# Result in four parts on two quadrants of two banks, V63 ending in parts of 8 keys, two pieces of K per VectorE instruction: a decode attention kernel on Trainium2

## The chip, the cores and the metric

One core of one Trainium2 chip. The metric is the device time of one execution in microseconds (us). The kernel before takes 1288.92 us (median of 3 runs, 1288.82 to 1288.93). Each kernel was also taken once with the hardware profiler; a profile's span is about 1.8 us shorter than the device time of the same execution.

## The reference, cut to what matters

```python
xn = layernorm(x)                                    # x: 4 x 512, one token for each of 4 batches
q  = (xn @ wq)                                       # 32 heads of 128
s  = einsum("bhqd,bhkd->bhqk", q, k_cache) * 128**-0.5   # 8192 keys a head
o  = einsum("bhqk,bhkd->bhqd", softmax(s), v_cache)
out = x + o.reshape(4, 1, 4096) @ wo + (silu(xn @ w_gate) * (xn @ w_up)) @ w_down
```

k_cache and v_cache are 4 x 32 x 8192 x 128 in bfloat16, 268 MB each. Everything is read once: 551 MB.

## The kernel before

The K and V caches go through five SBUF slots of 4 MB, one tile for two heads of one batch: 64 tiles K0 to K63 and 64 tiles V0 to V63. A stage i transposes K tile i on VectorE, multiplies it with q on TensorE (scores), takes the softmax of two tiles at a time, and multiplies V tile i - 2 with the probabilities (PV). wo takes one slot from stage 57 on. The parts that matter, with cuts marked:

```python
def t_piece(n, g):                       # one of 8 pieces of a K tile
    kt = kt_pool.tile([P, w], ...)       # 5 buffers
    nc.vector.transpose(out=kt..., in_=k_tiles[n][:, g * w:(g + 1) * w]...)
def s_piece(n, g):                       # 4 matmuls of 512 columns on that piece
    ...
# stage i, i < 64
for g in range(NTG):
    t_piece(i, g); s_piece(i, g)
...
# the parts in which V tiles are loaded
load_v(nv, (32, 32, 32, 16, 16) if nv == NT - 1 else (32,) * 4 if nv == NT - 2 else (T,))
...
# the last stage: V63, 128 keys, one matmul a key for batch 3, summed in xps
pv_last(xps, range(T // 2))
fin_2(H // HT - 1, xps, nb=B - 1, start=False)   # adds batches 0 to 2, from o_acc by ScalarE and VectorE
pv_last(xps, range(T // 2, T))
fin_3(H // HT - 1, xps)                          # otn, VectorE
...
def wo_mm(i):                                    # head i: 2 matmuls of 256 columns
    for half in range(2):
        mm(yo_ps[half][0:B, :], otn[:, i, :], wo_t[0][...half...], start=False)
...
nc.vector.tensor_copy(out=res[0][:], in_=yo_ps[0][0:B, :])
nc.sync.dma_start(out=out_flat[:, 0:DH], in_=res[0][:])
nc.scalar.copy(out=res[1][:], in_=yo_ps[1][0:B, :])
nc.scalar.dma_start(out=out_flat[:, DH:D], in_=res[1][:])
```

## Time and profile before

| | before |
|---|---|
| device time, median | 1288.92 us |
| span of the profile | 1287.1 us |
| TensorE / VectorE busy | 84% / 57% |
| DMA share, 100 to 1200 us | 1.00, 432 GB/s |
| last V part lands (chain of waits) | 1282.67 us |
| from there to the end of the span | 4.4 us |

The prediction below shows the page, the stretches and the timeline of the end, and says how to read each.

### The profile page before, as it was taken

How to read it: one execution, taken by the hardware profiler on the slowest of the kernel's cores; microseconds unless marked ns; L12 is line 12 of the kernel's file. 1: busy time of each engine (PE TensorE's matmuls, PEld its weight loads, DVE VectorE, ACT ScalarE, POOL GpSimd, SP SyncE). 2: the span in 40 equal slices, each digit the busy share in tenths (PEclk: the TensorE clock that was granted, in tenths of full speed). 3: DMA queues.
4: the chain of work that ended last, by engine and by line, in shares of the span. 5: the costliest groups of instructions: out<-in, count | busy, mean ns of one | idle time of the engine just before them, and what ended most of it. 6: DMA issues, size and time to landing. Idle time of an engine off the chain costs nothing.

```text
span 1287.1 us, 11189 instructions
## 1 busy us (share of the span) xinstructions
PE 1083.1 (84%) x4778; PEld 430.3 (33%) x4778; DVE 738.1 (57%) x951; ACT 39.7 (3%) x87; POOL 5.3 (0%) x13
## 2 busy tenths in 40 slices
PE   4888888888888798897997888888887988978788
PEld 1334333333333333332333333333333333333334
DVE  6663556546556556466556566465465465573544
ACT  1000000000000000000000000000000000000000
POOL 1000000000000000000000000000000000000000
PEclk9898898998989999898998989989899898989899
DMA  9999999999999999999999999999999999999997
GB/s 407 427 430 435 437 425 437 429 436 431 432 435 428 436 432 433 431 432 435 431 435 428 434 432 431 436 431 433 430 434 431 437 430 432 433 431 427 433 434 304
DMA packets 21529, 551.49 MB, mean 428 GB/s; under 512 B 2268, under 2 KB 2792, under 8 KB 3944
## 3 DMA queue, kind: packets, MB, share of 16 engines
q1 hardware_dynamic: 21464, 550.78, 99.4%
q8 instruction: 37, 0.61, 0.2%
q14 instruction: 12, 0.10, 0.0%
q10 hardware_dynamic: 16, 0.01, 0.0%
HBM read 550.77 MB, written 0.00 MB: 428 GB/s over the span
## 4 chain that ended last, share of the span: by engine, by line
DMA 50%; PE 31%; DVE 14%; issue 5%; ACT 1%; SPq 0%; DVEq 0%
DMA slot<-in_A_k_cache_dram 44%; PE oacc L76 17%; PE sps L76 12%; DVE kt L277 11%; DMA slot<-in_A_v_cache_dram 6%; PE mps L76 1%; DVE ptz L318 1%; DVE o L356 1%; PE xps L76 1%; DVE o_sb L354 1%; ACT o_sb L353 0%; PE mps L299 0%; DVE otn L377 0%; PE yo_ps L76 0%; DVE rcp L328 0%
## 5 line engine op out<-in xcount | busy, mean ns | idle before, releaser
L76 PE MATMUL sps<-kt,zq 128*128 128x512 bf16 x2048 | 578.3, 421 | 145.2 <-DVE kt L277 128.7
L277 DVE STREAM_TRANSPOSE kt<-slot 128x1024 uint32<-128x1024 uint32 x512 | 587.6, 1210 | 90.4 <-DMA slot<-in_A_k_cache_dram 89.5
L76 PE MATMUL oacc<-slot,ptz 128*8 128x512 bf16 x2016 | 450.4, 379 | 0.4 <-DMA slot<-in_A_v_cache_dram 0.4
L76 PEld LDWEIGHTS <-zq 128*128 128x128 bf16 x2048 | 212.0, 104 | 496.1 <-issue 317.0
L76 PEld LDWEIGHTS <-ptz 128*8 128x8 bf16 x2016 | 177.5, 92 | 258.1 <-issue 27.8
L328 DVE RECIPROCAL rcp<-mps 128x4 f32<-128x4 f32 x32 | 5.9, 183 | 281.9 <-PE mps L76 281.9
L354 DVE TENSOR_TENSOR o_sb<-o_sb,rowu 128x512 f32<-128x512 f32 x16 | 11.1, 693 | 89.2 <-ACT o_sb L353 89.0
L76 PE MATMUL xps<-rowy,o 128*32 128x4 f32 (+1 forms) x228 | 13.5, 205 | 37.3 <-DVE o L356 37.3
L293 DVE TENSOR_REDUCE mx<-sps 128x1 f32<-128x512 f32 x32 | 22.1, 692 | 18.5 <-PE sps L76 18.5
L76 PEld LDWEIGHTS xps<-rowy,o 128*32 128x32 f32 (+1 forms) x228 | 12.1, 154 | 44.9 <-DVE o L356 44.9
L268 DVE COPY zq<-qt 32x8 bf16<-32x8 bf16 x128 | 21.3, 166 | 1.3
L302 DVE TENSOR_REDUCE nm<-mps 128x4 f32<-128x64 f32 x32 | 7.2, 225 | 24.0 <-PE mps L299 24.0
L356 DVE TENSOR_REDUCE o<-o_sb 128x128 f32<-128x512 f32 x16 | 16.3, 1020 | 0.5
L76 PEld LDWEIGHTS mps<-rowb,rs 128*128 128x128 f32 x64 | 9.5, 186 | 13.8 <-issue 13.8
L76 PEld LDWEIGHTS <-slot 128*128 128x128 bf16 x272 | 11.7, 126 | 3.5 <-DVE slot L188 2.6
L76 PE MATMUL mps<-rowb,rs 128*128 128x4 f32 x64 | 12.3, 263 | 0.0
L353 ACT COPY o_sb<-oacc 128x512 f32<-128x512 f32 x16 | 9.4, 586 | 76.8 <-PE oacc L76 76.8
L377 DVE TENSOR_TENSOR otn<-xps,rcp 32x16 bf16<-32x16 f32 x28 | 4.8, 170 | 11.7 <-PE xps L76 10.3
L299 PE MATMUL mps<-ident_f,mx 128*128 128x128 f32 x32 | 10.3, 323 | 0.8 <-DVE mx L293 0.8
L299 PEld LDWEIGHTS mps<-ident_f,mx 128*128 128x128 f32 x32 | 4.3, 133 | 14.7 <-DVE mx L293 14.2
L170 PE MATMUL xps<-ident,kt 4*128 4x4 bf16 x4 | 0.3, 173 | 10.1 <-DVE kt L165 10.1
L76 PE MATMUL yo_ps<-slot,otn 128*4 128x256 bf16 x64 | 8.2, 281 | 0.3 <-DVE otn L366 0.3
(150 smaller groups left out, 148.5 us busy)
## 6 DMA issues: line engine op xcount, KB each, us to landing
slot<-in_A_k_cache_dram SPq DMA_DIRECT2D x64, 4096.0 KB, 39.2
slot<-in_A_v_cache_dram SPq DMA_DIRECT2D x62, 4096.0 KB, 36.8
slot<-in_A_v_cache_dram SPq DMA_DIRECT2D x7, 1024.0 KB, 22.3
slot<-in_A_wq_dram SPq DMA_DIRECT2D x1, 4096.0 KB, 12.3
slot<-in_A_wo_dram SPq DMA_DIRECT2D x1, 3584.0 KB, 40.2
slot<-in_B_w_gate_dram SPq DMA_DIRECT2D x1, 1792.0 KB, 31.9
slot<-in_B_w_up_dram SPq DMA_DIRECT2D x1, 1792.0 KB, 35.8
slot<-in_B_w_down_dram SPq DMA_DIRECT2D x1, 1792.0 KB, 30.9
```

The costliest lines, as they stand in the source:

```text
L76: nc.tensor.matmul(out_ap, lhsT=lhsT, rhs=rhs, start=start, stop=True, skip_group_check=True, **kw)
L268: nc.vector.tensor_copy(out=zq[gr % 2][a * QB:(a + 1) * QB, :, :, XO + a * QB].rearrange("p b (j r) -> p r j b", r=2), in_=qt[a * QB:(a + ...
L277: nc.vector.transpose(out=kt[:].bitcast(dt.uint32).rearrange("p (j t r) -> p t j r", j=2, r=QB), in_=src.rearrange("p (t j r) -> p t j r", ...
L293: nc.vector.reduce_max(out=mx[:], in_=s_ps[gr][:], axis=AX.X)
L299: nc.tensor.matmul(mps[:, 0:P], lhsT=nmx.pop(gr)[:, 0:1].to_broadcast([P, P]), rhs=ident_f[:, :], is_transpose=True, start=True, stop=True ...
L302: nc.vector.tensor_reduce(out=nm[:], in_=by_row(mps[:, 0:P]), axis=AX.XY, op=ALU.max, negate=True)
L318: nc.vector.transpose(out=t_[y * HP:(y + 1) * HP, :, y, :, :].rearrange("p s u x -> p s (u x)"), in_=p_[y * HP:(y + 1) * HP, :].rearrange( ...
L328: nc.vector.reciprocal(out=rcp[j][:, :, 2 * bp:2 * bp + 2], in_=mps[:, P:P + B].rearrange("p (y b) -> p y b", y=HT))
L353: nc.scalar.copy(out=o_sb[:].rearrange("p u d -> p (u d)"), in_=o_acc[j % 2][:])
L354: nc.vector.tensor_tensor(out=o_sb[:], in0=o_sb[:], in1=rowu[:].unsqueeze(2).to_broadcast([P, NV, Dh]), op=ALU.mult)
L356: nc.vector.reduce_sum(out=o1[:], in_=o_sb[:].rearrange("p u d -> p d u"), axis=AX.X)
L377: nc.vector.tensor_tensor(out=otn[q0:q1, blk * 4:blk * 4 + 4, :], in0=xps[q0:q1], in1=r_[q0:q1, y, :].unsqueeze(1).to_broadcast([QB, 4, B] ...
```

## The change

Its intent: shorten the serial end (fewer keys behind the last landing, two overlapping quadrants for the result product, narrower rounding copies on two engines) and save VectorE the fixed cost of half of its transposes (0.15 us each by the prediction's estimate). Buffers are cut to make room. The diff, cut to its core:

```diff
+    ND = 2
-    kt_pool = ctx.enter_context(tc.tile_pool(name="ktp", bufs=5))
+    kt_pool = ctx.enter_context(tc.tile_pool(name="ktp", bufs=3))
 ...
-    yo_ps = [psY.tile([B, DH], dt.float32, name="yo_ps") for _ in range(2)]
+    DH, DQ = D // 2, D // 4
+    yo_ps = [psY.tile([2 * QB, DQ], dt.float32, name="yo_ps") for _ in range(2)]   # and zeroed
+    def yo_mm(lhsT, rhs, start):
+        for i in range(2):
+            for a in range(2):
+                c0 = a * DH + i * DQ
+                mm(yo_ps[i][a * QB:a * QB + B, :], lhsT, rhs[:, c0:c0 + DQ], start=start)
 ...
-    def t_piece(n, g):
+    def t_piece(n, g, nd):          # nd pieces in one transpose
 ...
-        p_ = pp.tile([P, 512], dt.bfloat16, name="p_")
+        p_ = pp.tile([P, 512], dt.bfloat16, name="p_", bufs=1)      # o_sb likewise
 ...
-            load_v(nv, (32, 32, 32, 16, 16) if nv == NT - 1 ...
+            load_v(nv, (32, 32, 32, 16, 8, 8) if nv == NT - 1 ...
 ...
-            for g in range(NTG):
-                t_piece(i, g)
-                s_piece(i, g)
+            nd = 1 if i >= NT - 2 else ND
+            for k in range(0, NTG, nd):
+                t_piece(i, k, nd)
+                for g in range(k, k + nd):
+                    s_piece(i, g)
 ...
-    (the two copies and two stores shown above)
+    res = persist.tile([2 * QB, DH], dt.bfloat16, name="res")
+    nc.vector.tensor_copy(out=res[:, 0:DQ], in_=yo_ps[0][:])
+    nc.scalar.copy(out=res[:, DQ:DH], in_=yo_ps[1][:])
+    nc.sync.dma_start(out=out_flat[:, 0:DH], in_=res[0:B, :])
+    nc.scalar.dma_start(out=out_flat[:, DH:D], in_=res[QB:QB + B, :])
```

More of the change, by code (lines that the diff above doesn't have):

```diff
@@ L203 @@
     otn = persist.tile([P, H, B], dt.bfloat16, name="otn")
-    DH = D // 2
-    yo_ps = [psY.tile([B, DH], dt.float32, name="yo_ps") for _ in range(2)]
+    DH, DQ = D // 2, D // 4
+    yo_ps = [psY.tile([2 * QB, DQ], dt.float32, name="yo_ps") for _ in range(2)]
+    for y_ in yo_ps:
+        nc.vector.memset(y_[:], 0.0)
+    def yo_mm(lhsT, rhs, start):
[3 more added lines that the diff above has]
+                mm(yo_ps[i][a * QB:a * QB + B, :], lhsT, rhs[:, c0:c0 + DQ], start=start)
     ffn = {}
@@ L240, in do_ffn @@
         nc.vector.tensor_tensor(out=yfx[:], in0=yf_ps[0:B, :], in1=xf[:], op=ALU.add)
-        for j in range(2):
-            mm(yo_ps[j][0:B, :], ident_f[0:B, 0:B], yfx[:, j * DH:(j + 1) * DH], start=True)
+        yo_mm(ident_f[0:B, 0:B], yfx[:], True)
     NB4 = H // 4
@@ L270, in build_q @@
                 in_=qt[a * QB:(a + 1) * QB, half, :, hh * 2:hh * 2 + 2, cg * B + bp * 2:cg * B + bp * 2 + 2])
-    def t_piece(n, g):
+    def t_piece(n, g, nd):
         w = TG * Dh
-        kt = kt_pool.tile([P, w], dt.bfloat16, name="kt")
-        src = k_tiles[n][:, g * w:(g + 1) * w].bitcast(dt.uint32)
-        nc.vector.transpose(out=kt[:].bitcast(dt.uint32).rearrange("p (j t r) -> p t j r", j=2, r=QB),
+        kt = kt_pool.tile([P, ND * w], dt.bfloat16, name="kt")
+        src = k_tiles[n][:, g * w:(g + nd) * w].bitcast(dt.uint32)
+        nc.vector.transpose(out=kt[:, 0:nd * w].bitcast(dt.uint32).rearrange("p (j t r) -> p t j r", j=2, r=QB),
                             in_=src.rearrange("p (t j r) -> p t j r", j=2, r=QB))
-        kts[n, g] = kt
+        for i in range(nd):
+            kts[n, g + i] = kt[:, 0:nd * w].rearrange("p (j n r) -> p j n r", j=2, r=2)[:, :, i * 512:(i + 1) * 512, :]
     def s_piece(n, g):
@@ L284, in s_piece @@
             s_ps[gr] = psS.tile([P, 512], dt.float32, name="sps")
-        kt = kts.pop((n, g))[:].rearrange("p (j n r) -> p j n r", j=2, r=2)
+        kt = kts.pop((n, g))
         off = XO - 2 * (bb * NTG + g)
@@ L351, in fin_1 @@
     def fin_1(j):
-        o_sb = pp.tile([P, NV, Dh], dt.float32, name="o_sb")
+        o_sb = pp.tile([P, NV, Dh], dt.float32, name="o_sb", bufs=1)
         nc.scalar.copy(out=o_sb[:].rearrange("p u d -> p (u d)"), in_=o_acc[j % 2][:])
@@ L380, in wo_mm @@
     def wo_mm(i):
-        for half in range(2):
-            mm(yo_ps[half][0:B, :], otn[:, i, :], wo_t[0][:, i * D + half * DH:i * D + (half + 1) * DH], start=False)
+        yo_mm(otn[:, i, :], wo_t[0][:, i * D:(i + 1) * D], False)
     NK = T // NV
@@ L394 @@
         if 0 <= nv < NT:
-            load_v(nv, (32, 32, 32, 16, 16) if nv == NT - 1 else (32,) * 4 if nv == NT - 2 else (T,))
+            load_v(nv, (32, 32, 32, 16, 8, 8) if nv == NT - 1 else (32,) * 4 if nv == NT - 2 else (T,))
         if i == R_FFN - 3:
@@ L403 @@
         if i < NT:
-            for g in range(NTG):
-                t_piece(i, g)
-                s_piece(i, g)
-                if g == 0 and bb == 0 and gr > 0:
+            nd = 1 if i >= NT - 2 else ND
[3 more added lines that the diff above has]
+                    s_piece(i, g)
+                if k == 0 and bb == 0 and gr > 0:
                     pt_turn(gr - 1)
@@ L453 @@
     assert wo_next == H
-    res = [persist.tile([B, DH], dt.bfloat16, name=f"res{j}") for j in range(2)]
-    nc.vector.tensor_copy(out=res[0][:], in_=yo_ps[0][0:B, :])
-    nc.sync.dma_start(out=out_flat[:, 0:DH], in_=res[0][:])
-    nc.scalar.copy(out=res[1][:], in_=yo_ps[1][0:B, :])
-    nc.scalar.dma_start(out=out_flat[:, DH:D], in_=res[1][:])
+    res = persist.tile([2 * QB, DH], dt.bfloat16, name="res")
[3 more added lines that the diff above has]
+    nc.scalar.dma_start(out=out_flat[:, DH:D], in_=res[QB:QB + B, :])
 _INS = ['A_x', 'A_k_cache', 'A_v_cache', 'A_wq', 'A_wo', 'B_x', 'B_w_gate', 'B_w_up', 'B_w_down']
```

## The prediction

The cost of 1.4 us a fetch is an estimate, 0.93 + 1.7 - 1.213. What the query projection "agrees" with is that quadrants work at the same time. The trace shows it: each of its 32 matmuls lasted 0.59 to 0.63 us, and all of them together 3.61 us. The 0.04 us in the result product's sum is the author's estimate.

> **What bounds the kernel now.** I read the page first (the 40 slices, the DMA queues, the costliest groups), then the waits, then stretches of time at the end, then the timeline of the last 5 us.
>
> ```profile
> span 1287.1 us, 11189 instructions
> DMA  9999999999999999999999999999999999999997
> q1 hardware_dynamic: 21464, 550.78, 99.4%
> q8 instruction: 37, 0.61, 0.2%
> L277 DVE STREAM_TRANSPOSE kt<-slot 128x1024 uint32<-128x1024 uint32 x512 | 587.6, 1210 | 90.4 <-DMA slot<-in_A_k_cache_dram 89.5
> slot<-in_A_k_cache_dram SPq DMA_DIRECT2D x64, 4096.0 KB, 39.2
> slot<-in_A_v_cache_dram SPq DMA_DIRECT2D x62, 4096.0 KB, 36.8
> ```
>
> The reader is to see that the DMA engines are full in every slice but the last: 550.78 MB, 99.4% of the time of 16 engines. VectorE is busy 57% and TensorE 84%, and VectorE's transposes themselves wait for K (89.5 us of their 90.4 us of idle time). A 4 MB tile alone needs 4.19 MB / 432 GB/s = 9.7 us, yet takes 37 to 39 us from issue to landing: about four tiles stand in the queue, so some 29 us of earlier work lie ahead of each issue.
>
> The stretches (core us, then busy of PE, weight load, VectorE, ScalarE, GpSimd, then granted clock, DMA share, GB/s):
>
> ```profile
> 100.00:1200.00 1100.00, 932.77 (x3984) 367.92 (x3983) 629.97 (x812) 30.23 (x71) 0.00 (x0) 0.93 1.00 432
> 1268.00:1275.00 7.00, 7.00 (x38) 3.06 (x37) 1.08 (x2) 0.00 (x0) 0.00 (x0) 1.00 0.99 418
> 1275.00:1279.00 4.00, 4.00 (x45) 2.07 (x44) 0.43 (x2) 0.59 (x1) 0.00 (x0) 1.00 0.57 242
> 1279.00:1281.00 2.00, 1.51 (x52) 1.42 (x49) 1.48 (x2) 0.00 (x0) 0.00 (x0) 1.00 0.51 203
> 1281.00:1282.00 1.00, 1.00 (x44) 1.00 (x41) 0.00 (x0) 0.00 (x0) 0.00 (x0) 0.62 0.25 102
> ```
>
> For 1100 us the stream runs flat at 432 GB/s. From 1275 us on only half of the engines still work: they do not finish together. In the trace's DMA records 16,150 of the 16,256 packets of 32,768 B took 1.212 or 1.213 us, whatever else ran, so no other work slows the stream. [...] each of the 37 packets of 16,384 B in q8 took about 0.93 us, and the data packet beside it about 1.7 us in place of 1.213, so one costs its engine about 1.4 us. The completion packets of the last V part end at about 1275 us on the fastest engines and at 1281.7 to 1282.4 us on the five slowest. [...]
>
> The timeline of the end:
>
> ```profile
> 1282.71 0.59 PE L76 MATMUL xps<-ptz,slot 128*128 128x2 bf16 x16 [0.48 <-DMA slot<-in_A_v_cache_dram]
> 1283.34 0.17 DVE L366 TENSOR_TENSOR otn<-xps,rcp 128x8 bf16<-128x8 f32 x1 [2.83 <-PE xps L76]
> 1283.56 1.01 PE L76 MATMUL yo_ps<-slot,otn 128*4 128x256 bf16 x4 [0.26 <-DVE otn L366]
> 1284.40 0.41 DVE L456 CAST res<-yo_ps 4x256 bf16<-4x256 f32 x1 [0.89 <-PE yo_ps L76]
> 1284.61 0.36 ACT L458 CAST res<-yo_ps 4x256 bf16<-4x256 f32 x1 [5.89 <-PE yo_ps L76]
> 1284.84 0.35 SPq L457 DMA_DIRECT2D out_dram<-res  x1
> 1285.00 0.28 ACTq L459 DMA_DIRECT2D out_dram<-res  x1
> ```
>
> The last V part lands at 1282.67 us (the chain of waits), and everything after it is serial: 4.4 us to the end of the span, of which 2.1 us lie after ScalarE's copy (1284.97 us).
>
> [...] The query projection agrees:
>
> ```profile
> 13.05 3.61 PE L76 MATMUL sps<-slot,xnt_w 128*32 128x512 bf16 x32 [2.66 <-DMA slot<-in_A_wq_dram]
> ```
>
> Its 32 matmuls of 512 columns into four quadrants took 3.61 us, 0.11 us each[...].
>
> **The change part by part.**
>
> Two pieces of K per VectorE instruction. 62 of the 64 tiles take 4 transposes of 128x2048 in place of 8 of 128x1024: 248 instructions fewer. VectorE's casts from PSUM took 1,220 ns for 1024 elements and 691 for 512, so 1.03 ns an element; of a transpose's 1,210 ns 1,058 are then elements and about 0.15 us is fixed. A pair should take 1.21 + 1.06 = 2.27 us, and 248 x 0.15 = 37 us go from the sum of durations (512 x 1.21 = 620 us to about 582). Neighbours overlap (eight take 9.1 us, 1.14 each), so of the busy time, 588 us, some 25 us go. None is on the path: VectorE waits for DMA already. The price: the first matmul of a tile waits about 2.3 us for the first pair, not 1.2 us, and after the last transpose 8 matmuls (1.7 us) remain, not 4. So TensorE may end each stage about 1 us later. A stage is 2 x 9.7 = 19.4 us of DMA; TensorE's work in it is about 32 x 0.28 + 32 x 0.21 = 16 us, and a slot freed 1 us later meets 29 us of queue. Worth 0. The smaller pools (three double buffers are six pieces against five; one buffer for the probabilities and for the scaled output) are released within a stage, well before their next writer. Worth 0. The last two tiles keep single pieces, so the end is prepared as before. Two memsets at the start lie in VectorE's wait for the first K: 0.
>
> V63's last 16 keys as 8 and 8. Packets of 8 keys are 2,048 B. Those of 16 keys take 159 ns and those of 1,024 B 46 ns, so about 84 ns: 16 x 84 against 8 x 159, plus a completion packet, is +0.08 us on the slowest engine. After the landing 8 matmuls remain in place of 16: 0.59 us becomes about 0.30, -0.29 us. The program's order shows that the new last part waits for the landing of a DMA eight places earlier, now the second part of V62: issued near 1268 us instead of 1265.5. The fastest engine is busy with V63 until 1275, so it costs nothing.
>
> The result matrix product. 4 matmuls of 256 columns become 8 of 128, alternating between two quadrants. Now: starts 0.203 us apart, one lasts 0.42 us, of which 256 columns are 0.21 (half of the 0.43 us that 512 took in the projection; the granted clock is 0.50 here); 3 x 0.203 + 0.42 = 1.03 us. After, if the two quadrants overlap as in the query projection: 3 x 0.107 + 0.04 + (0.42 - 0.107) = 0.67 us, -0.36 us. The two rounding copies fall from 256 to 128 columns: ScalarE takes 586 ns for 512 columns and 362 for 256, 0.875 ns a column, so 0.25 for 128: -0.11 us. VectorE's, about 0.28 us, starts two matmuls earlier and is hidden. Both result DMAs now wait for both copies, but the later one waited for ScalarE's anyway: 0.
>
> [...]
>
> Sum: +0.08 - 0.29 - 0.36 - 0.11 = -0.68 us. 1288.92 - 0.68 = 1288.24, taken as 1288.2.
>
> **The rivals.** (1) The DMA skew moves. A fetch more or less on the slowest engine is +-1.4 us, twice the gain. For it: [...] the last fell at 1280.65 us, 2 us before the end. [...] It would make 1287.5 to 1289.6. (2) The quadrants do not overlap: then 7 x 0.107 + 0.31 = 1.06 us, +0.03 in place of -0.36; the time would be 1288.6. Against: the projection. (3) The pairs slow the steady state by holding K slots longer, or starving TensorE: with 64 tiles 1 us each would be 64 us, 1350. Against: 29 us of queued DMA ahead of each issue, and flat 432 GB/s. (4) VectorE's saving shows as time: 25 us, 1264. Against: VectorE idles for K already. I give (3) and (4) one chance in a hundred each or less.
>
> **Range and chances.** Runs before differ by 0.11 us. The terms of the end can be off by 0.3 us, the skew by about 1: 1287.2 to 1289.4. The 2% threshold is 25.8 us, far beyond anything at the end (the whole tail after the last landing is 4.4 us): within 2%: 0.98.
>
> **What would show it.** The DMA slices stay at 9 and 432 GB/s; transposes 264 in all (248 of about 2.27 us, 16 of 1.21), some 563 us busy; the last V landing within 0.4 us of 1282.7; 8 last matmuls in 0.3 us; 8 result matmuls in about 0.67 us; copies of 0.28 and 0.25 us; a span near 1286.4 us. Wrong would be: DMA gaps in the steady part, a landing off by over 1 us (skew), or 1.0 us for the result matmuls (no overlap).

## The result, and the profile after

The changed kernel took 1288.84 us (median of 6 runs, 1288.57 to 1288.93); the kernel before in the same rounds 1288.91 (6 runs, 1288.59 to 1288.95). The ratio, the mean time of one kernel's runs over that of the other's of the same rounds (so not quite the ratio of the medians), is 0.9999, with an interval of 0.9987 to 1.0012: the same. The time lies in the predicted range. But the prediction had summed 0.68 us of gain and the two profiles have the same span. So the question is where 0.7 us went.

The page of the changed kernel, the lines that answer to those of before (span, DMA slices, fetches, transposes):

```profile
span 1287.1 us, 10897 instructions
DMA  9999999999999999999999999999999999999997
q8 instruction: 38, 0.62, 0.2%
L286 DVE STREAM_TRANSPOSE kt<-slot 128x2048 uint32<-128x2048 uint32 (+1 forms) x264 | 572.6, 2218 | 56.0 <-DMA slot<-in_A_k_cache_dram 55.1
```

The stream is as full as it was, and VectorE's transposes fell by 15 us of busy time without any effect on the span. Now the last steps of the chain of waits, first of the kernel before, then of the changed one (start, duration, what):

```profile
1265.54 17.13 DMA slot<-in_A_v_cache_dram
1282.67 0.05 issue
1282.71 0.60 PE xps L76 x16
```

```profile
1266.99 12.01 PE oacc L77 x59
1279.00 0.02 issue
...
1280.42 1.05 DVE o L366
1281.46 0.04 issue
1281.51 2.07 PE xps L77 x66
```

This is the reading that matters most. Before, the chain comes from a DMA: TensorE waits for the last V part. After, no DMA stands in it. TensorE ends PV of V62 late, ScalarE and VectorE work on its sum, then TensorE has 66 matmuls left (the two of `fin_2` and the whole second half of V63), 2.07 us, while the last V part had long landed. By the landing records it came at 1282.46 us, and TensorE was done only at 1283.58.

The timeline of the end after, to set beside the one in the prediction:

```profile
1281.75 1.82 PE L77 MATMUL xps<-ptz,slot 128*128 128x2 bf16 x64
1283.61 0.17 DVE L376 TENSOR_TENSOR otn<-xps,rcp 128x8 bf16<-128x8 f32 x1 [2.15 <-PE xps L77]
1283.83 0.59 PE L77 MATMUL yo_ps<-slot,otn 128*4 128x128 bf16 x8 [0.26 <-DVE otn L376]
1284.35 0.28 DVE L468 CAST res<-yo_ps 64x128 bf16<-64x128 f32 x1 [0.58 <-PE yo_ps L77]
1284.46 0.26 ACT L469 CAST res<-yo_ps 64x128 bf16<-64x128 f32 x1 [4.80 <-PE yo_ps L77]
1284.74 0.35 SPq L470 DMA_DIRECT2D out_dram<-res  x1
1284.74 0.28 ACTq L471 DMA_DIRECT2D out_dram<-res  x1
```

The result product and the copies did become shorter, by just about what was predicted. The account of the end, from these lines and the landing records:

| step | predicted | before, us | after, us | measured change |
|---|---|---|---|---|
| last V part lands | +0.08 | at 1282.67 | at 1282.46 | -0.21 |
| from there to the last matmul on V63 | -0.29 | 0.64 | 1.12 | +0.48 |
| to the start of the result matmuls | 0 | 0.25 | 0.25 | 0 |
| result matmuls | -0.36 | 1.03 | 0.61 | -0.42 |
| ScalarE's copy, with its start | -0.11 | 0.38 | 0.28 | -0.10 |
| from its end to the end of the span | 0 | 2.14 | 2.39 | +0.25 |
| sum | -0.68 | | | 0.00 |

Two terms went wrong: TensorE was late (0.48 in place of -0.29), and the stores took 0.25 us longer.

When did TensorE become late? The starts of the transposes of the last K tiles, and of ScalarE's copy that follows PV of V62, give the length of each stage (us, from each kernel's timeline; the experiments below are in the same table; where "V62's sum" has a time below, it is the start of that copy):

| kernel | K60 starts | stage 60 | stage 61 | stage 62 | stage 63 to the copy | copy starts |
|---|---|---|---|---|---|---|
| before | 1195.28 | 19.47 | 20.56 | 19.14 | 23.68 | 1278.13 |
| changed | 1194.95 | 19.81 | 21.43 | 19.14 | 23.74 | 1279.07 |
| pairs only | 1194.72 | 20.02 | 21.22 | 19.13 | 23.75 | 1278.84 |
| pairs in all tiles | 1194.65 | 19.81 | 21.39 | 19.80 | 24.41 | 1280.06 |
| changed, wo early | 1194.66 | 19.80 | 21.23 | 19.13 | 23.75 | 1278.57 |
| single in the last 4 | 1194.70 | 19.45 | 20.56 | 19.75 | 23.74 | 1278.20 |
| single in all | 1195.28 | 19.52 | 20.56 | 19.94 | 23.75 | 1279.05 |
| single in all, clock held | 1195.15 | 19.64 | 20.56 | 19.14 | 23.74 | 1278.23 |

In the changed kernel stages 60 and 61, the last two with pairs, took 0.34 and 0.87 us longer. Up to K60 TensorE has slack: it waited 10.4 us before its first score matmul of K60 in the kernel before. From there on the last four tiles of K and the PV that belongs to them run one behind the other into the end, with hardly a wait for the stream. In the kernel before this serial work was ready only 0.48 us ahead of the last landing.

One thing goes the other way. K60 started between 1194.65 and 1194.95 us in all six profiles with pairs in the middle tiles, and between 1195.05 and 1195.46 in the seven without (leaving out the run with more instruction fetches). So the pairs bring the start of the serial part forward by some 0.5 us, and the last two of them cost about 1.0 to 1.2 us behind it. Why K60 lands earlier was not tested.

### The profile page after: what moved, and what is told of

It reads as the page before. It is cut to its first block, busy times and chain, and to the rows that moved or that the text cites. A ratio compares the mean times of both kernels' runs of the same rounds, so it can differ in the third digit from the quotient of the medians.

```text
span 1287.1 us, 10897 instructions
## 1 busy us (share of the span) xinstructions
PE 1049.1 (82%) x4783; PEld 430.0 (33%) x4846; DVE 722.1 (56%) x705; ACT 39.5 (3%) x87; POOL 5.3 (0%) x13
## 4 chain that ended last, share of the span: by engine, by line
DMA 48%; PE 30%; DVE 18%; issue 3%; ACT 0%; SPq 0%; DVEq 0%; ACTq 0%
DMA slot<-in_A_k_cache_dram 48%; PE oacc L77 18%; DVE kt L286 17%; PE sps L77 10%; PE mps L77 1%; DVE ptz L328 1%; PE mps L309 0%; PE xps L77 0%; DVE o L366 0%; DVE o_sb L364 0%; ACT o_sb L363 0%; DVE rcp L338 0%; DVE yfx L250 0%; PE yo_ps L77 0%; DVE sig L242 0%
## 5 line engine op out<-in xcount | busy, mean ns | idle before, releaser
L77 PE MATMUL sps<-kt,zq 128*128 128x512 bf16 x1985 | 547.3, 421 | 179.9 <-DVE kt L286 169.1
L286 DVE STREAM_TRANSPOSE kt<-slot 128x2048 uint32<-128x2048 uint32 (+1 forms) x264 | 572.6, 2218 | 56.0 <-DMA slot<-in_A_k_cache_dram 55.1
L77 PE MATMUL xps<-rowy,o 128*32 128x4 f32 (+1 forms) x228 | 13.7, 206 | 37.3 <-DVE o L366 37.3
L77 PE MATMUL mps<-slot,ht 128*4 128x512 bf16 x14 | 5.8, 600 | 1.6 <-DVE ht L246 1.6
```

The lines of the kernel that those rows point to most:

```text
L77: nc.tensor.matmul(out_ap, lhsT=lhsT, rhs=rhs, start=start, stop=True, skip_group_check=True, **kw)
L286: nc.vector.transpose(out=kt[:, 0:nd * w].bitcast(dt.uint32).rearrange("p (j t r) -> p t j r", j=2, r=QB), in_=src.rearrange("p (t j r) -> ...
```

## The experiments

Theory A: the pairs in K60 and K61 delay TensorE, and TensorE, not the last landing, sets the end. Rivals: the result matmuls or K60's landing make it late (B), pairs in the middle save something (C), the stores eat any gain (D). Device times below are medians; "before" is always the kernel before in the same rounds. In these sessions its own runs scatter over 0.8 to 0.95 us (1288.73 to 1289.66 in the first), so what is settled below a microsecond is settled by the traces, not by the medians. The first four experiments ran on one chip, the others on another.

### Single pieces in the last four tiles

```diff
-            nd = 1 if i >= NT - 2 else ND
+            nd = 1 if i >= NT - 4 else ND
```

> The changed kernel with single pieces of K in the last four tiles, not only the last two. Theory A (the pairs in K60 and K61 lengthened the serial work of TensorE and VectorE at the end by about 1.2 us, so the last matmuls on V63 no longer wait for the last landing but for TensorE): TensorE is done with PV of V62 within 0.3 us of 1278.0, the 8 last matmuls wait for the last V part, the chain of waits ends in that DMA again, the end is 3.8 to 3.9 us after that landing in place of 4.43, span about 1286.4 us, time 1288.2 (about 0.6 us below before). Rival B (the eight result matmuls a head or a later landing of K60 made TensorE late, not the pairs): PV of V62 still ends near 1278.9 and the time stays at 1288.8.

Measured: 1288.25 us (1287.76 to 1288.64, 5 runs), before 1289.27; span 1286.5 us. V62's sum was ready at 1278.20 as theory A said, 0.87 us earlier than in the changed kernel, of which 0.25 us is K60's earlier start, and stages 60 and 61 have the length that they have in the kernel before, with the result matmuls as changed: rival B falls as the main cause. The time fits. But the chain did not end in the DMA again: the part landed at 1282.18 and the last matmul on V63 ended at 1282.95. And stage 62, which is the same in code, took 19.75 us in place of 19.14. Something else costs 0.6 us there.

### Single pieces in all tiles

```diff
-    ND = 2
+    ND = 1
-    kt_pool = ... bufs=3
+    kt_pool = ... bufs=5
```

> The changed kernel with single pieces in all 64 tiles (five buffers again); the result layout and the V63 parts as changed. Theory A: the same as with single pieces in the last four tiles, 1288.2, and pairs elsewhere are worth nothing. Rival C (the pairs in the middle save some time through VectorE's 15 us less busy time): 0.3 us or more slower than the run with single pieces in the last four only.

Measured: 1288.45 us (1288.17 to 1289.09, 5 runs), before 1289.27; span of the profiled one, the slowest of the five, 1287.3. It is 0.2 us slower than the run before it, less than rival C asked for and well within the scatter, so the device times show no worth of pairs in the middle and do not exclude a small one: K60 started 0.58 us later here. Stages 60 and 61 are again those of the kernel before, but stage 62 took 19.94 us: 0.80 too long, with not a pair in the kernel. Theory A alone does not explain this profile.

### Pairs in all tiles

```diff
-            nd = 1 if i >= NT - 2 else ND
+            nd = ND
```

> The changed kernel with pairs in the last two tiles too. Theory A: each pair-wise tile on the serial end adds about 0.9 us (first wait 2.3 us in place of 1.2, measured +0.87 for K61), so TensorE ends the matmuls on V63 about 1.8 us later than in the changed kernel and the time is about 1290.6 (1289.9 to 1291). If TensorE's lateness has another cause, the time stays within 0.3 us of 1288.8.

Measured: 1289.85 us (1289.80 to 1290.05, 4 runs), before 1289.27; span 1288.1. Stages 62 and 63 became longer by 0.66 and 0.67 us, and the last matmul on V63 ended at 1284.59, 1.0 us later than in the changed kernel; the span grew by 1.0. The direction and the mechanism are theory A's. (The granted clock was 0.50 from 1235.3 to 1242.1 us, in stage 62. It is not what made that stage longer: before its last 8 score matmuls TensorE waited for VectorE's transpose again, and stage 63, at a clock of 1.00, grew by as much.) The size was expected too high: 0.66 us a tile, not 0.9.

### The pairs alone, on the kernel before

The edit: the diff above without the result's four parts and without the parts of 8 keys (the smaller pools go with the pairs).

> The kernel before with only the pairs of K (and the smaller pools that go with them). Theory A: TensorE about 0.9 us late at the end, of which 0.48 us is its wait for the last landing in before, so the last matmuls on V63 end 0.3 to 0.5 us later and the time is about 1289.3. Rival B: the same as before, 1288.9.

Measured: 1288.87 us (1288.69 to 1289.10, 4 runs), before 1289.27 with its scatter; span 1287.3 against 1287.1 of the profile of before. V62's sum came at 1278.84, 0.71 us later than before, and the last matmul on V63 ended at 1283.53, 0.2 later. The stages grew by 0.55 and 0.66 us. The trace agrees with theory A in sign; the effect on the end was below the 0.3 to 0.5 expected, as K60 had landed 0.56 us earlier, and the medians show no loss at all. By itself this run settles little.

### wo loaded earlier

```diff
-        if i == R_WO - 2:
+        if i == 24:
             load_wo()
```

On the changed kernel, on the one with single pieces, and on the kernel before:

> The changed kernel (pairs in 62 tiles, result in four parts, V63 in parts of 8) with the load of wo moved from stage 57 to stage 24, so that K60 is not held up behind it and TensorE enters the last stages ahead. Theory A (TensorE's serial work from K60 on sets the end): PV of V62 ends some us before 1278, the last 8 matmuls wait for the last V part, which lands at 1282.2 to 1282.7; from there 3.85 us to the end, span about 1286.3, time 1288.1 (0.7 to 1.0 below the kernel before of the same rounds), whatever the pairs. Rival D (the end is set by the last landing in any case, and the gain is lost in the stores): no change from 1288.8.

> As the run before, with single pieces of K in all tiles. Theory A: the same time as with pairs, within 0.2 us, since neither pairs nor clock reach the path when TensorE is ahead.

> The kernel before with only the load of wo moved to stage 24. Its last 16 matmuls waited 0.48 us for the landing already, so theory A expects no gain: the same 4.4 us from the landing to the end and the same time as before within 0.3 us. If the time falls by 0.6 us, the early load itself is worth it and not the changed end.

Measured: 1288.62 (1288.38 to 1288.70, 5 runs), 1288.65 (1288.24 to 1288.89, 5) and 1288.69 us (1288.67 to 1288.75, 4), before 1289.35 (1288.71 to 1289.63). The reasoning behind these three was wrong. K60 started at 1194.66, 1195.46 and 1195.14 us, no earlier than in the other profiles: wo is in the stream ahead of K60 whether early or late, and the stream is what counts. TensorE's wait at K60 only moved to earlier stages, and it was not ahead at the end: V62's sum came at 1278.57, 1278.52 and 1277.94. The first two end in TensorE's matmuls, not in the landing (last matmul on V63 at 1283.06 and 1283.25, landings at 1282.59 and 1282.82). The third waited 0.51 us for its landing at 1282.46 and ended 4.4 us after it, as the kernel before did, so an early wo is worth nothing that can be told from scatter. The run with pairs is useful all the same: with no fall of the clock in the last 99 us before 1282 (below), its stages 60 and 61 are 0.33 and 0.67 us longer than before's. That is the cost of the pairs alone: 1.0 us (0.41 and 0.65 against the kernel before with wo early).

### The clock held up

Stage 62 of the single-piece runs had to be explained. The stretches around the end of stage 61 (the column after GpSimd's is the granted clock), first of the kernel before, then of the one with single pieces in all tiles:

```profile
1235.00:1239.00 4.00, 3.04 (x22) 1.77 (x22) 3.75 (x5) 0.00 (x0) 0.00 (x0) 1.00 0.95 410
1239.00:1243.00 4.00, 3.65 (x15) 1.35 (x15) 4.00 (x5) 0.00 (x0) 0.00 (x0) 1.00 1.14 492
```

```profile
1235.00:1239.00 4.00, 2.67 (x37) 1.60 (x39) 3.69 (x5) 0.00 (x0) 0.00 (x0) 0.75 1.01 434
1239.00:1243.00 4.00, 3.78 (x9) 1.26 (x9) 4.00 (x5) 0.00 (x0) 0.00 (x0) 0.50 1.04 451
```

From 1237.0 to 1243.8 us the granted clock was 0.50. But for the last one, which the end of the program cuts off, the half-clock stretches of these profiles last 3.4, 6.8, 10.2 or 13.7 us; in the clock records of the kernel before (26 stretches) and of the changed one (37) each is a whole multiple of 3.413 us, and so are those at 1.00 between them. So the 3.4 us before a fall are what is compared here. At the end of stage 61 TensorE waits about 2.45 us for VectorE's sum, and then runs the result matmuls of 8 heads: 1.91 us before, 1.06 us with the overlapped quadrants. The 3.4 us before the fall, 1233.6 to 1237.0, have 1.73 us of TensorE work in them, so TensorE was not idle; the like stretch of the kernel before, where the clock stayed at 1.00, has 2.00. Theory E, a guess, says that this short work let the clock fall, and that the fall made stage 62 longer. Its test puts more work there:

```diff
             if bv == B - 1 or npv == NT - 2:
                 fin_1(jv)
+            if i == NT - 3:
+                for _ in range(12):      # result unused; yo_ps made 512 columns wide
+                    mm(yo_ps[0][0:B, DQ:512], ident[:, 0:B], qt_flat[:, 0:384], start=False)
```

> The changed kernel with single pieces in all tiles (as the run without pairs) and 12 idle matmuls of 384 columns on TensorE in the wait at the end of stage 61, their result unused. Clock theory E (TensorE's short work there let its granted clock fall to 0.50 for 3.4 to 6.8 us near 1235 us, which cost stage 62 its 0.6 to 0.8 us): no half-clock stretch near 1235 us, stage 62 again 19.1 us from transpose to transpose in place of 19.75 to 19.94, V62's PV done 0.6 to 0.8 us earlier, about 1278.3 after a K60 at 1195.3. If the clock still falls or the stage stays long, theory E is wrong.

Measured: 1288.34 us (1288.22 to 1288.54, 4 runs), before 1289.35; span 1286.5. The same stretches of this run:

```profile
1235.00:1239.00 4.00, 2.29 (x38) 1.49 (x39) 3.70 (x5) 0.00 (x0) 0.00 (x0) 1.00 1.01 434
1239.00:1243.00 4.00, 3.61 (x14) 1.34 (x14) 4.00 (x5) 0.00 (x0) 0.00 (x0) 1.00 1.08 467
```

The clock stays at 1.00 and stage 62 takes 19.14 us again; V62's sum came at 1278.23, and the chain of waits ends in the DMA again: the last V part landed at 1282.58, and the 8 matmuls behind it took 0.39 us. So one half of theory E holds: without the fall stage 62 has its old length. The other half, why the clock fell and what held it, is not shown. The stretches of 3.4 us lie nearly as in the run without the added matmuls (ends at 1237.1 and 1237.0), and the last run below repeats the result; but the 12 matmuls ran from 1231.4 to 1233.5 us, before the stretch in question (1233.7 to 1237.1, with 1.84 us of work against 1.73) and not in the wait, which they only cut from 2.45 to 1.36 us. Nor do short result matmuls decide alone: the run with wo early and pairs had the short 1.06 us and no fall, while the kernel before with wo early and the run with pairs only had the long ones and a fall of 3.4 us. Nor is TensorE's busy time alone the measure: the clock fell after stretches of 3.4 us with 0.95 (before, wo early), 1.02 (changed), 1.38 (single in the last 4) and 1.73 us (single in all) of TensorE work, and stayed after others with 1.52 (changed, wo early), 1.84 and 2.00 us. Falls of 6.8 us came only with the short ones, in three profiles of nine (in two of the nine the added matmuls ran). In the changed kernel the clock fell for 3.4 us at 1235.4; its stage 61 is 0.20 us longer than in the run with pairs and no fall. The fall at the very end counts too: with single pieces in the last four tiles the clock was 0.50 from 1280.3 us on and the last 66 matmuls on V63 took 2.31 us, against 2.07 in the changed kernel, whose clock fell at 1283.1.

### The order of the last matmuls

If TensorE's queue is the bound, then the place of `fin_2` matters: it waits for ScalarE and VectorE, and half of V63 stands behind it. On the changed kernel, pairs and all:

```diff
-            pv_last(xps, range(T // 2))
+            pv_last(xps, range(T - 16))
             fin_2(H // HT - 1, xps, nb=B - 1, start=False)
-            pv_last(xps, range(T // 2, T))
+            pv_last(xps, range(T - 16, T))
```

> The changed kernel with one line of order moved: the two matmuls that add the other three batches' sums (they wait for ScalarE's and VectorE's work on V62's result, done near 1281.5) stand before the last 16 keys of V63, not before its second half of 64. Theory A: TensorE has then only 16 matmuls left after them and waits for the last landing again (1282.4 to 1282.8): 8 matmuls in 0.3 us, 3.85 us from the landing to the end, span 1286.3 to 1286.6, 0.4 to 0.7 us below the changed kernel, with the pairs and the clock as they were. If the lateness of TensorE is not what holds the end, no change.

Measured: 1288.23 us (1287.76 to 1288.89, 5 runs), before 1288.78 (1288.55 to 1289.36); span 1286.7, 0.4 below the changed kernel's. V62's sum came late as in the changed kernel (1278.88), and the clock fell as there, but 112 matmuls were done before `fin_2`, and the chain waits for the DMA again:

```profile
1267.31 15.48 DMA slot<-in_A_v_cache_dram
1282.78 0.05 issue
1282.83 0.38 PE xps L77 x8
```

Eight matmuls are left, 0.38 us (0.30 expected). From the landing at 1282.78 to the end it is 3.96 us (4.44 before, 4.64 in the changed kernel; 3.85 expected). This is the direct test of theory A's second half, that TensorE sets the end in the changed kernel, and it holds in the trace: with nothing changed but the order, the landing is the bound again and the span falls by 0.4 us. The device times agree in sign, but their ranges overlap.

### All remedies together

Single pieces, the 12 added matmuls (the clock stayed at 1.00 in the run with them; that they held it is not shown) and the moved order, on the changed result layout and V63 parts:

> All found remedies in one: single pieces of K, idle matmuls that hold the clock at the end of stage 61, and the moved order, on the changed result layout and V63 parts. Theory A: bounded by the last landing as the run with the moved order alone, within 0.2 us of it, 1288.0 to 1288.3; nothing more is to be had from TensorE. If it is over 0.3 us faster than that run, TensorE was still on the path there.

Measured: 1288.22 us (1288.12 to 1288.41, 5 runs), before 1288.78 (1288.55 to 1289.36, 9 runs); span 1286.4. The ranges do not meet: about 0.5 us below the kernel before, though the interval of the ratio (0.9983 to 1.0008) includes 1. It is also below the changed kernel's 1288.84, which was measured in another session. Its landing was at 1282.49, 0.29 earlier than in the run with the moved order alone, which is the whole difference of their spans: the medians are equal, and TensorE is off the path in both. The plain order change is the simpler remedy; this version scatters less.

### Two questions on the side

The prediction put the lag of some DMA engines at the end (from about 1275 to 1282.4 us, some 7 us) down to TensorE's instruction fetches, estimated at 1.4 us each. On the kernel before:

```diff
+        if 6 <= i < 50:
+            for _ in range(24):          # result unused
+                mm(yo_ps[0][0:B, DH:DH + B], ident[:, 0:B], ident[:, 0:B], start=False)
```

> The kernel before with 24 small matmuls more in each of the stages 6 to 49 (1,056 matmuls of 4 columns and their 1,056 weight loads, result unused): 2,112 TensorE instructions[...]. If instruction fetches are what makes eight DMA engines late at the end (the prediction's reading of the skew), q8 shows 45 or 46 packets in place of 37, [...] the last V part lands 1.4 us later, near 1284.0, and the time rises by 1.2 to 1.6 us against before of the same rounds. Rival: if the skew has another cause, the landing stays within 0.4 us of 1282.6 and the time within 0.4 us.

Measured: 1289.87 us (1289.78 to 1289.98, 4 runs), before 1288.78; span 1288.1.

```profile
q8 instruction: 45, 0.74, 0.2%
```

Eight more fetches (the profile of before has 37 packets for its 9,556 TensorE matmuls and weight loads, 258 to a packet, so 8 for 2,112 more agree with it), and the last V part lands at 1283.63 in place of 1282.67: 0.97 us later, below the 1.4 expected, and the time rises by 1.1. So the fetches do cost time in a full stream. The packets' own times account for it: the fetches and the packets of 32,768 B that took over 1.3 us cost 14.9 us more in all than in the kernel before, 0.93 us for each of 16 engines, or 1.86 us a fetch. That they explain the lag between engines is not shown: the quarter of V63's packets of 4,096 B that ended first was done 0.73 us later too (1274.64 against 1273.91), so the lag itself grew by 0.24 us only. What makes the rest of the 7 us stays open.

The other question is the 0.25 us behind ScalarE's copy. In the changed kernel each store reads columns that both engines wrote, so both are issued at 1284.74. From issue to landing SP's took 1.43 us there and 1.20 before; ScalarE's 1.25 and 1.22. Behind the store that lands last, SP's sequencer then has two more waits to check at the program's end, 0.06 us each, where before it had one. All nine profiles with this result layout in which both stores left within 0.01 us look alike, and none with the old layout does. The test on the kernel before:

```diff
-    nc.vector.tensor_copy(out=res[0][:], in_=yo_ps[0][0:B, :])
+    for c in range(2):
+        c0, c1 = c * DH // 2, (c + 1) * DH // 2
+        nc.vector.tensor_copy(out=res[0][:, c0:c1], in_=yo_ps[0][0:B, c0:c1])
```

> The kernel before, with VectorE's rounding copy cut into two of 128 columns, so that it ends about 0.15 us later, just when ScalarE's ends, and both result stores are issued at nearly the same time, as in the changed kernel. If stores issued at one time delay each other, SP's store takes about 1.42 us from issue to landing in place of 1.20, ScalarE's stays near 1.2, and the end comes 0.15 to 0.25 us later than its ScalarE copy would give in before (2.13 us from that copy's end to the end of the span becomes about 2.3). If not, both take 1.20 and the 2.13 stays.

Measured: 1288.82 us (1288.79 to 1288.94, 4 runs), before 1288.78; span 1287.1. The experiment failed in its setup: the two short copies overlapped and took 0.48 us, not 0.56, so the stores were issued at 1284.80 and 1284.90, still 0.10 us apart. They took 1.20 and 1.28 us. It decides nothing; the collision of the two stores is a reading of the profiles, not shown by an experiment.

## Why the prediction was right or wrong

- The time and its class were right: 1288.84 us in the range 1287.2 to 1289.4, within 2%, since the stream of 551 MB at 432 GB/s is untouched and the whole end is 4.4 us. That the exact time fell into the range owes something to luck: the range was drawn for a skew of the DMA engines, and the miss of 0.6 us came from elsewhere. Rivals (3), as a loss in every stage, and (4) did not happen: VectorE's 15 us less busy time bought nothing.
- The predicted gain of 0.68 us did not come, and the step that failed is in the first part: a slot freed later meets a deep queue, "Worth 0", and "The last two tiles keep single pieces, so the end is prepared as before." The reasoning was about loads and holds for them. It missed that from K60 on there is hardly any load left to hide behind: the stages run serially into the end. The prediction itself said that TensorE may end a stage 1 us later; in stages 60 and 61 this was 0.33 and 0.67 us (the run without a clock fall), and it reached the end. The warning was in the timeline it showed: TensorE's wait for the last landing was 0.48 us, so a delay of TensorE by more than that makes TensorE the bound in place of the DMA.
- "After the landing 8 matmuls remain", -0.29 us: wrong for the same reason. TensorE had 66 left at 1281.51. Where the DMA was the bound again, the 8 took 0.38 us.
- The result matmuls in two quadrants, -0.36 us: right, -0.42 measured. Rival (2), no overlap, falls. The two quadrants were at work at the same time: 8 matmuls of 128 columns, 0.26 to 0.31 us each, took 0.61 us, where one after another they would have needed 1.06 by the prediction's estimate. ScalarE's copy, -0.11: right, -0.10.
- "Both result DMAs now wait for both copies, but the later one waited for ScalarE's anyway: 0": wrong, +0.25 us, with the stores issued together.
- The last landing: +0.08 predicted, -0.21 measured, inside the skew of about 1 us that was allowed for. Over the profiles with the changed result layout and V63 parts it lies between 1282.2 and 1282.8. Rival (1) was rightly kept open and did not decide.
- VectorE: a pair took 2.28 us (2.27 predicted), 264 transposes, 573 us busy (some 563 predicted).
- Two sizes in the prediction's working were off without effect. A fetch cost 1.86 us in the experiment, not 1.4. And the lower end of rival (1), 1287.5, is not 1.4 us below 1288.2.
- A side effect that nobody predicted: TensorE's clock fell at the end of stage 61. It cost 0.20 us in the changed kernel and 0.6 to 0.8 us in two of the experiments. That the shorter result matmuls brought it about is not shown.

## What to carry to other kernels

In this kernel, with the DMA share at 1.00, VectorE's 15 us of busy time were worth nothing while loads lay behind them, and 0.33 and 0.67 us more in stages 60 and 61, with hardly a load behind them, reached the end. So find the last point where an engine waits for the stream (here 10.4 us, before the first score matmul of K60), and treat all that follows as one serial path, on which a coarser instruction is paid for: a first transpose of 2.28 us in place of 1.21 cost 0.33 to 0.67 us a tile here. Before shortening the last steps, read how long the engine waited there for the landing, since that slack (0.48 us here) is all that may be lost elsewhere; and keep what depends on other engines as late as possible in TensorE's program order (here 112 matmuls on V63 in place of 64 before `fin_2` took the span from 1287.1 to 1286.7 us). And look at the granted clock of each stage before comparing its length: in two runs here a fall of 6.8 us made stage 62 longer by 0.6 to 0.8 us, with the same code in it.
